# Retention attention with a Mish feed-forward layer: a new order of the first steps, and loads issued later in a visit

## The chip, the cores and the metric

The kernel runs on one core of a Trainium2 chip. The metric is device time in microseconds (us), the median of several runs. A separate execution under the hardware profiler gives the profile; its times are read against that execution's own time.

Engines are named as in the profile: PE is TensorE (matrix products; PEld its weight loads), DVE is VectorE, ACT is ScalarE, POOL is GpSimd, SP is SyncE, which here only issues DMAs. "L371" is line 371 of the kernel's file.

## The reference

Two stages are computed. The first is retention: per batch and head, scores q k^T / sqrt(64) are multiplied by a decay mask and then with v. The second takes the result as 4608 tokens of 512 features through a feed-forward layer with Mish, h tanh(softplus(h)).

```python
def _attn_ref(q, k, v):                 # (8, 8, 576, 64) each
    scores = scale * np.matmul(q, k.transpose(0, 1, 3, 2))
    gamma = 1.0 - 2.0 ** (-5.0 - np.arange(H))
    rel = pos[:, None] - pos[None, :]
    Dmat = np.where(rel >= 0, gamma[:, None, None] ** rel[None, :, :], 0.0)
    return np.matmul(scores * Dmat[None], v)

def _moe_ref(x, w_in, w_out):           # (4608, 512), (512, 2048), (2048, 512)
    h = x @ w_in
    sp = np.where(h > 20.0, h, np.log1p(np.exp(np.minimum(h, 20.0))))
    return (h * np.tanh(sp)) @ w_out
```

## The kernel before

**Tiling.** The 4608 tokens are 36 chunks of 128, four of them (c = 4) half from one batch and half from the next. Four chunks make a tile of 512 tokens, so there are nine tiles t. The order is: first the first 128 positions of all eight batches (tiles 0 and 1, "first" chunks, numbered 0 to 7), then for each pair of batches the chunks 1 to 3 of both and the shared last one (chunks 8 to 35). A first chunk needs only the masked scores. A later chunk also needs a state, the sum of k^T v over the earlier positions of its batch.

**Order.** The schedule is written out by hand: each engine carries out its instructions in the order in which the program emits them, and waits only where data or a buffer is missing. So moving a Python line moves its instructions in the queues of all engines that it uses.

**Helpers for the first chunks** (t is 0 or 1, g the half: batches 0 and 1, or 2 and 3; i is 0 for q, 1 for k). `f_transpose(t, g, i, parts)` transposes on PE into PSUM (L194, L197) and copies to SBUF (L202) with the engine that `parts` names. `f_scores(t, g)` makes the scores of two batches on PE (L211) and multiplies each by `dmask` on VectorE (L215). `f_v(t, b, copy)` casts v of a batch to bf16 (L222). `f_out(t, b, copy)` multiplies masked scores with v (L236) and casts the result into the tile `xT` (L239). `f_state` scales v for the state (L245). `keep_warm(n, pool, name)` issues n matrix products of zeros (L167) into a PSUM buffer of a pool; nobody reads them. The pools `ps_sc` and `ps_h` have two buffers each, `ps_st` and `ps_o` one.

**Feed-forward.** `g1(t, f)` is one of 16 blocks of the first product, four matmuls (L371), with the Mish on ScalarE (L373). With `half[0]` or `half[1]` it does 256 of the 512 token columns: for tile 0 the blocks 0 to 3 are done by halves, the first half needing `xT` of batches 0 and 1 only. `g2(t, i)` is a quarter of the second product of one chunk, four matmuls (L386); `g2_first` does the same for tile 0 (L403), `g2_last` (L414) for the last chunk. `store` copies the result out of PSUM (L422) and issues the store on SP.

**Tables on ScalarE.** `dmask`, `gq` and `gv` are exponentials (Exp), `gq` and `gv` made from `ex`, which VectorE computes from `pos`; `warm` is a single Mish on one column, whose effect is that the Mish table is loaded there.

**First loads.** q of batches 0 to 3 is issued by SP (L120), k of them by POOL (L106), v by POOL in pairs of batches (L117), then w_in in four blocks (L86).

**Later chunks.** `load(n)` issues q, k and v of a chunk on POOL (L263; L267 for the shared chunks): into `qraw` (5 buffers), `qks` (9) and `vraw` (7). Steps of a chunk: P scales q on VectorE (L273), V scales v on POOL (L279, into `vs`, 5 buffers), T transposes q and k, on PE (L288, copy L289) for chunks under 18 and as a DMA transpose issued by SP (L291) from 18 on, S makes the scores (L301) and masks them (L305), O adds state and scores times v (L353, L358) and casts to `xT` (L362). `state` makes the next state (L333, L336). `load_k0(b)` loads k of a batch's first chunk again (L249).

**The main loop** (t = 2 to 9) does 16 steps per tile, in two visits of eight (w = 0 to 7). A visit works on chunks n and n+1: S at w = 0, O at w = 4, and for the next pair the V, T and P steps. Each step also does one `g1` of tile t and one `g2` of tile t-1. `more_loads(upto)` issues the loads that are still missing up to chunk `upto`, at most two; PF = 5 is how far ahead they run. In tiles 3 and 4, `load_k0` stands at the top of steps 4 and 12.

Of the kernel before, what the change touches and what calls it, by code (L numbers as in the profile page):

```python
# [17 lines left out]
def kernel(  # L18
# [29 lines left out]
    PF = 5  # L48
# [23 lines left out]
    ps_sc = ctx.enter_context(tc.tile_pool(name="ps_sc", bufs=2, space=PS))  # L72
    ps_st = ctx.enter_context(tc.tile_pool(name="ps_st", bufs=1, space=PS))
    ps_h = ctx.enter_context(tc.tile_pool(name="ps_h", bufs=2, space=PS))
    ps_o = ctx.enter_context(tc.tile_pool(name="ps_o", bufs=1, space=PS))
# [21 lines left out]
    q0 = gts[0][:, H:nF, :].bitcast(F32).rearrange("p (b a) c -> p b (a c)", a=2)  # L97
    v0 = {}
    fst = {}
# [64 lines left out]
    def keep_warm(n, pool=ps_o, name="ops"):  # L164
        idle = pool.tile([P, 512], F32, name=name)
        for _ in range(n):
            nc.tensor.matmul(idle, lhsT=zeros[:, 0:P], rhs=zeros, start=True, stop=True)  # L167
# [14 lines left out]
    def f_transpose(t, g, i, parts):  # L182

        name = ("qb", "kb")[i]
        out_t = first.tile([P, H, P], BF16, name=name + "T", bufs=2)
        n = 8 // len(parts)
        moves = []
        for j, (pool, tname, copy) in enumerate(parts):
            tp = pool.tile([P, 2, 8, P] if tname == "sc" else [P, 8, P], BF16, name=tname)
            tp = (tp[:, 0] if tname == "sc" else tp)[:, 0:n]  # L190
            for r in range(n):
                if t == 1:
                    mix = fst[1][name, "mix", g][:, n * j + r]
                    nc.tensor.transpose(tp[:, r, :], mix.rearrange("p x d -> p (x d)"), ident)  # L194
                else:
                    for x in range(2):
                        nc.tensor.transpose(tp[ds(64 * x, 64), r, :],  # L197
                                            fst[0][name][:, 2 * g + x, ts(n * j + r, D)], ident)
            moves.append((copy, out_t.rearrange("p h (g r) -> p h g r", r=8)[:, :, :, ds(n * j, n)],
                          tp.rearrange("p r (g h) -> p h g r", h=H)))  # L200
        for copy, to, src in moves:
            copy(to, src)  # L202
        fst[t][name, g] = out_t

    def f_scores(t, g, between=None):
        qT, kT = fst[t]["qb", g], fst[t]["kb", g]
        scs = [ps_sc.tile([P, 2, NP, P], F32, name="sc").rearrange("p a b i -> p (a b) i") for _ in range(2)]
        for h in range(H):
            for x in range(2):
                r = ds(64 * x, 64)  # L210
                nc.tensor.matmul(scs[x][:, h, :], lhsT=kT[r, h, :], rhs=qT[r, h, :], start=True, stop=True)  # L211
        for x in range(2):
            b = 2 * g + x
            sm = first.tile([P, H, P], BF16, name="sm0", bufs=4)
            nc.vector.tensor_tensor(sm, scs[x], dmask, op=OP.mult)  # L215
            fst[t]["sm", b] = sm
            if between and x == 0:
                between()

    def f_v(t, b, copy):  # L220
        vb = first.tile([P, H, D], BF16, name="vb", bufs=4)
        copy(vb, v0[4 * t + b])  # L222
        fst[t]["vb"][b] = vb

    def f_out(t, b, copy):
        if b == 0:
            xts[t] = xp.tile([P, KC, NCH * P], BF16, name="xT")
        vb = fst[t]["vb"][b]
        if t == 0:
            pool, name = ((ps_h, "hp"), (ps_h, "hp"), (ps_st, "st"), (ps_o, "ops"))[b]  # L230
            ot = pool.tile([P, NP, P], F32, name=name)
        else:
            ot = ps_sc.tile([P, 2, NP, P], F32, name="sc")[:, 0]
        for p in range(NP):
            for e in range(2):
                nc.tensor.matmul(ot[ds(64 * e, 64), p, :], lhsT=vb[:, 2 * p + e, :],  # L236
                                 rhs=fst[t]["sm", b][:, 2 * p + e, :],
                                 start=(p == 0), stop=True, skip_group_check=True)
        copy(xts[t][:, :, ts(b, P)], ot)  # L239
# [7 lines left out]
    def load_k0(b):  # L247
        k0[b] = first.tile([P, H, D], BF16, name="k0", bufs=B)
        nc.gpsimd.dma_start(out=k0[b], in_=k[b, :, 0:P, :].rearrange("h p d -> p h d"))  # L249
# [3 lines left out]
    def load(n):  # L253
        if n >= n_chunks:
            return
        b, c = chunks[n]
        qr = io.tile([P, H, D], F32, name="qraw")
        vr = io.tile([P, H, D], F32, name="vraw", bufs=7)
        qks = io.tile([P, 2, H, D], BF16, name="qks", bufs=9)
        live[n] = {"q": qr, "v": vr, "qks": qks}  # L260
        for t, src in ((qr, q), (qks[:, 1], k), (vr, v)):
            if c < 4:
                nc.gpsimd.dma_start(  # L263
                    out=t, in_=src[b, :, ds(P * c, P), :].rearrange("h p d -> p h d"))
            else:
                for e in range(2):
                    nc.gpsimd.dma_start(  # L267
                        out=t[ds(64 * e, 64)],
                        in_=src[b + e, :, ds(512, 64), :].rearrange("h p d -> p h d"))
# [123 lines left out]
    def stores():  # L393
        while ready:
            store(*ready.pop(), nc.vector.tensor_copy)
# [34 lines left out]
    def att(n, steps):  # L430
        if n >= n_chunks:
            return
        for step in steps:
            {"P": step_p, "V": step_v, "T": step_t, "S": step_s, "O": step_o}[step](n)

    dve, act, pool = nc.vector.tensor_copy, nc.scalar.copy, nc.gpsimd.tensor_copy
# [1 line left out]

    half = (slice(0, 2 * P), slice(2 * P, 4 * P))
    nc.scalar.activation(dmask, dmask, AX.Exp, bias=lnd[:, 0:1])  # L440
    for b in range(2):
        dve(fst[0]["qb"][:, b, :], q0[:, b, :])
    keep_warm(8)
    f_transpose(0, 0, 1, [(ps_h, "hp", act), (ps_h, "hp", dve)])
    f_transpose(0, 0, 0, [(ps_st, "st", act), (ps_o, "ops", dve)])
    for h in range(H):
        nc.vector.tensor_scalar(ex[:, :, h], pos, lg[h], None, op0=OP.mult)
    act(fst[0]["qb"][:, 2, :], q0[:, 2, :])
    f_transpose(0, 1, 1, [(ps_h, "hp", act), (ps_h, "hp", act)])
    keep_warm(2, ps_sc, "sc")  # L450
    f_scores(0, 0)
    keep_warm(3, ps_st, "st")
    f_transpose(0, 1, 0, [(ps_st, "st", act), (ps_o, "ops", act)])
    keep_warm(4, ps_h, "hp")
    nc.scalar.activation(gq, ex, AX.Exp)
    nc.scalar.activation(gv, ex, AX.Exp, scale=-1.0)
    nc.scalar.activation(warm, lnd, AX.Mish)
    f_v(0, 0, pool)
    f_v(0, 1, pool)
    f_scores(0, 1, lambda: f_out(0, 0, dve))  # L460
    f_out(0, 1, act)
    f_v(0, 2, pool)
    f_v(0, 3, act)
    keep_warm(3, ps_st, "st")
    for f in range(4):
        g1(0, f, half[0])
# [34 lines left out]
    for i in range(nF):  # L501
        for step in steps.get(i, "").split():
            n = int(step[1])
# [17 lines left out]
    def more_loads(upto):  # L521
        for _ in range(2):
            if queued[0] <= upto:
                load(queued[0])
                queued[0] += 1
# [4 lines left out]
    for u in range(24):  # L530
        j, w = divmod(u, 4)
# [32 lines left out]
    for t in range(2, nT + 1):  # L564
        for i in range(nF):
            n, w = NCH * (t + 1) + i // 8 * 2, i % 8
            if t in (3, 4) and i in (4, 12):
                load_k0(2 * t - 2 + i // 8)
            by_pe = n + 2 < NPE
            if w == 0:  # L570
                stores()
                state(n + 1)
                att(n, "S")
                att(n + 1, "S")
            if w == 4:
                state(n + 3)
                stores()
                att(n, "O")
                att(n + 1, "O")
                state(n + 3)  # L580
            if by_pe and w in (1, 3):
                att(n + 2 + w // 2, "P")
            if w in (0, 1):
                att(n + 2 + w, "V")
                more_loads(n + 2 + w + PF)
            if w - (5 if by_pe else 0) in (0, 1):
                att(n + 2 + (w == 1 or w == 6), "T")
            if w == 7 and n + 4 >= NPE:
                att(n + 4, "P")
                att(n + 5, "P")  # L590
            stores()
            if t < nT:
                g1(t, i)
            if t == 2:
                if i % 2:
                    g2(1, 8 + i // 2)
            elif t < nT or i < 12:
                g2(t - 1, i)
# [32 lines left out]
```

## Time and profile before

| what | us |
|---|---|
| three runs | 315.39, 315.41, 316.31 (median 315.41) |
| the profiled execution's own time | 317.75 |
| its span, first to last instruction | 316.0 |
| PE busy in 0 to 20 us of the span | 14.24 |
| PE busy in 20 to 40 | 19.02 |
| PE busy in 120 to 140 | 19.55 |
| PE busy in 140 to 160 | 18.78 |
| PE busy in 180 to 200 | 19.90 |

Except in the last 16 us, other stretches of 20 us hold between 19.79 and 19.90 us of PE work. The difference of 1.75 us between the profiled time and the span lies before the first and after the last recorded instruction.

How to read it. The page cuts the span into 40 slices of 7.9 us and gives each engine's busy share as a digit (9 is 90 per cent or more). PEclk is the clock that was granted to TensorE, in tenths of full speed; DMA is the busy share of the 16 DMA engines. A timeline row has the start, the duration, the engine, the line and the instruction, and in brackets how long the engine had been idle before and who released it. A matmul's recorded duration includes its drain, so a row of x16 is a little longer than the pace of the stream.

Transfers, from issue to landing: the last pair of v for tile 0 was issued at 7.1 us and took 9.3; the four blocks of w_in were issued at 6.4, 9.3, 10.1 and 10.8 and took 7.7, 9.2, 12.0 and 13.9; w_out was issued at 19.1, 20.9, 29.1 and 30.1 and took 10.8, 11.6, 8.4 and 10.1.

### The profile page before, as it was taken

How to read it: one execution, taken by the hardware profiler on the slowest of the kernel's cores; microseconds unless marked ns; L12 is line 12 of the kernel's file. 1: busy time of each engine (PE TensorE's matmuls, PEld its weight loads, DVE VectorE, ACT ScalarE, POOL GpSimd, SP SyncE). 2: the span in 40 equal slices, each digit the busy share in tenths (PEclk: the TensorE clock that was granted, in tenths of full speed). 3: DMA queues.
4: the chain of work that ended last, by engine and by line, in shares of the span. 5: the costliest groups of instructions: out<-in, count | busy, mean ns of one | idle time of the engine just before them, and what ended most of it. 6: DMA issues, size and time to landing. Idle time of an engine off the chain costs nothing.

```text
span 316.0 us, 5807 instructions
## 1 busy us (share of the span) xinstructions
PE 302.7 (96%) x2428; PEld 153.4 (49%) x2468; DVE 135.3 (43%) x198; ACT 111.7 (35%) x185; POOL 143.0 (45%) x178
## 2 busy tenths in 40 slices
PE   5779999999999999998999999999999999999995
PEld 2454554555555554544545454545454545444444
DVE  3553148487636535353535453535354332001111
ACT  3476525753353533332232333332323232333300
POOL 8587849889684976356373536252010000000000
PEclk9599999999999999999999999999999999999999
DMA  7999999999992899999999999991514000010031
GB/s 176 232 207 204 221 207 197 274 163 183 234 183 79 139 163 164 187 83 210 153 181 88 214 136 180 122 168 36 98 37 100 35 33 35 34 33 33 35 97 69
DMA packets 73642, 42.85 MB, mean 136 GB/s; under 512 B 58640, under 2 KB 64528, under 8 KB 73616
## 3 DMA queue, kind: packets, MB, share of 16 engines
q0 software_dynamic: 48640, 27.27, 64.0%
q1 hardware_dynamic: 24832, 15.08, 25.9%
q8 instruction: 19, 0.31, 0.5%
q10 hardware_dynamic: 144, 0.13, 0.1%
q14 instruction: 7, 0.06, 0.1%
HBM read 38.80 MB, written 9.44 MB: 153 GB/s over the span
## 4 chain that ended last, share of the span: by engine, by line
PE 74%; DMA 20%; POOL 3%; issue 1%; ACT 0%; DVE 0%; POOLq 0%
PE hp L371 31%; PE ops L386 26%; DMA qkT<-qks 9%; PE hp L386 4%; DMA w_out_t<-in_moe_w_out_dram 4%; DMA qraw<-in_q_dram 4%; PE sc L301 2%; DMA vraw<-in_v_dram 2%; PE st L333 2%; DMA gT<-in_k_dram 2%; PE sc L353 1%; PE sc L358 1%; PE sc L288 1%; PE hp L414 1%; POOL gT L106 1%
## 5 line engine op out<-in xcount | busy, mean ns | idle before, releaser
L371 PE MATMUL hp<-xT,w_in_t 128*128 128x512 bf16 (+1 forms) x562 | 141.4, 373 | 2.9 <-DVE xT L239 0.8
L373 ACT ACTIVATE gT<-hp 128x512 bf16<-128x512 f32 (+1 forms) x148 | 86.8, 586 | 157.7 <-PE hp L371 143.9
L386 PE MATMUL ops<-w_out_t,gT 128*128 128x512 bf16 x430 | 110.1, 379 | 0.4
L371 PEld LDWEIGHTS <-w_in_t 128*128 128x128 bf16 x592 | 55.1, 98 | 62.8 <-issue 2.1
L386 PEld LDWEIGHTS <-gT 128*128 128x128 bf16 x496 | 48.3, 98 | 58.0 <-issue 0.8
L422 DVE COPY res<-ops 128x512 f32<-128x512 f32 x28 | 19.3, 688 | 83.4 <-PE ops L386 79.6
L336 DVE TENSOR_TENSOR ssb<-st,diag 128x512 bf16<-128x512 f32 x32 | 21.9, 685 | 49.6 <-PE st L333 49.6
L263 POOL DMA_DIRECT2D qraw<-in_q_dram x24 | 22.1, 921 | 40.5 <-DVE qks L273 38.0
L279 POOL TENSOR_TENSOR vs<-vraw,gv 128x512 bf16<-128x512 f32 x28 | 29.9, 1077 | 20.2 <-issue 14.0
L305 DVE TENSOR_TENSOR sm<-sc,mask 128x1024 bf16<-128x1024 f32 x28 | 33.1, 1216 | 5.9 <-PE sc L301 5.9
L263 POOL DMA_DIRECT2D vraw<-in_v_dram x24 | 21.7, 903 | 2.6 <-DMA vpair<-in_v_dram 1.5
L263 POOL DMA_DIRECT2D qks<-in_k_dram x24 | 21.6, 899 | 1.2 <-DMA w_out_t<-in_moe_w_out_dram 0.9
L273 DVE TENSOR_TENSOR qks<-qraw,gq 128x512 bf16<-128x512 f32 x28 | 19.9, 746 | 0.0
L362 DVE CAST xT<-sc 128x512 bf16<-128x512 f32 x24 | 15.3, 680 | 0.0
L386 PE MATMUL hp<-w_out_t,gT 128*128 128x512 bf16 x61 | 14.7, 379 | 0.2
L215 DVE TENSOR_TENSOR sm<-sc,dmask 128x1024 bf16<-128x1024 f32 x8 | 9.5, 1220 | 8.4 <-PE sc L211 8.4
L289 ACT COPY qkT<-sc 128x1024 bf16<-128x1024 bf16 x10 | 10.1, 1010 | 8.0 <-PE sc L288 8.0
L267 POOL DMA_DIRECT2D qraw<-in_q_dram x8 | 5.6, 708 | 14.1 <-DVE qks L273 14.1
L301 PE MATMUL sc<-qkT 64*128 64x128 bf16 x224 | 9.4, 218 | 1.5 <-DMA qkT<-qks 1.5
L301 PEld LDWEIGHTS <-qkT 64*128 64x128 bf16 x224 | 6.3, 94 | 6.7 <-issue 3.4
L353 PE MATMUL sc<-qkT,ssb 128*64 128x128 bf16 (+1 forms) x224 | 9.5, 213 | 0.0
L358 PE MATMUL sc<-sm,vs 128*64 128x128 bf16 x192 | 9.4, 219 | 0.0
(102 smaller groups left out, 193.3 us busy)
## 6 DMA issues: line engine op xcount, KB each, us to landing
out_dram<-res SPq DMA_DIRECT2D x31, 256.0 KB, 3.9
qraw<-in_q_dram POOLq DMA_DIRECT2D x24, 256.0 KB, 5.5
vraw<-in_v_dram POOLq DMA_DIRECT2D x24, 256.0 KB, 8.3
qks<-in_k_dram POOLq DMA_DIRECT2D x24, 128.0 KB, 7.3
w_in_t<-in_moe_w_in_dram POOLq DMA_DIRECT2D x4, 512.0 KB, 10.6
w_out_t<-in_moe_w_out_dram POOLq DMA_DIRECT2D x4, 512.0 KB, 10.4
gT<-in_q_dram SPq DMA_DIRECT2D x4, 256.0 KB, 4.9
gT<-in_k_dram POOLq DMA_DIRECT2D x8, 128.0 KB, 6.9
```

Of the source, the lines that this page charges most:

```text
L263: nc.gpsimd.dma_start(out=t, in_=src[b, :, ds(P * c, P), :].rearrange("h p d -> p h d"))
L273: nc.vector.tensor_tensor(live[n]["qks"][:, 0], live[n]["q"], gq[:, c, :].unsqueeze(2).to_broadcast([P, H, D]), op=OP.mult)
L279: nc.gpsimd.tensor_tensor(vs, live[n]["v"], gv[:, c, :].unsqueeze(2).to_broadcast([P, H, D]), op=OP.mult)
L301: nc.tensor.matmul(sc[:, e, p, :], lhsT=qk[r, 1, p, :], rhs=qk[r, 0, p, :], start=True, stop=True)
L305: nc.vector.tensor_tensor(sm.rearrange("p e n i -> p (e n) i"), sc.rearrange("p e n i -> p (e n) i"), m.unsqueeze(1).to_broadcast([P, 2 * ...
L336: nc.vector.tensor_tensor(ssb.rearrange("p e n d -> p e (n d)"), st.rearrange("p n d -> p (n d)").unsqueeze(1).to_broadcast([P, 2, NP * 64 ...
L353: nc.tensor.matmul(ot[ds(64 * e, 64), p, ds(i0, iw)], lhsT=st_sb[bb, cc][:, e, p, :], rhs=qk[:, 0, p, ds(i0, iw)], start=(i0 == 0 and p == ...
L362: nc.vector.tensor_copy(xts[t][:, :, ts(s, P)], ot)
L371: nc.tensor.matmul(hp[:, cols], lhsT=w_in_t[:, c, ts(f, P)], rhs=xts[t][:, c, cols], start=(c == 0), stop=(c == KC - 1))
L373: nc.scalar.activation(gts[t][:, f, cols], hp[:, cols], AX.Mish)
L386: nc.tensor.matmul(ops, lhsT=gts[t][:, f, ts(s, P)], rhs=w_out_t[:, f, :], start=(f == 0), stop=(f == nF - 1))
L422: copy(ot, ops)
```

## The change

It has two parts. In the first steps, ScalarE's `gq`, `gv` and the Mish table come right after `dmask`, and `ex` on VectorE moves ahead with them; the casts of q for batches 0 and 1 are no longer adjacent, and the cast of batch 2 goes from ScalarE to VectorE. The scores of the first half come ahead of the second half's transposes. The v casts of batches 0 to 2 stand together, the outputs of batches 0 and 1 ahead of the second half's scores, and the cast of batch 3 goes from ScalarE to VectorE. The warm-up matmuls change from 8, 2, 3, 4, 3 to 12, 2, 3, 3. In the main loop, the calls of `more_loads` go from steps 0 and 1 to steps 4 and 5 of a visit, for the same chunks.

```diff
     half = (slice(0, 2 * P), slice(2 * P, 4 * P))
     nc.scalar.activation(dmask, dmask, AX.Exp, bias=lnd[:, 0:1])
-    for b in range(2):
-        dve(fst[0]["qb"][:, b, :], q0[:, b, :])
-    keep_warm(8)
-    f_transpose(0, 0, 1, [(ps_h, "hp", act), (ps_h, "hp", dve)])
-    f_transpose(0, 0, 0, [(ps_st, "st", act), (ps_o, "ops", dve)])
+    dve(fst[0]["qb"][:, 0, :], q0[:, 0, :])
     for h in range(H):
         nc.vector.tensor_scalar(ex[:, :, h], pos, lg[h], None, op0=OP.mult)
-    act(fst[0]["qb"][:, 2, :], q0[:, 2, :])
-    f_transpose(0, 1, 1, [(ps_h, "hp", act), (ps_h, "hp", act)])
-    keep_warm(2, ps_sc, "sc")
-    f_scores(0, 0)
-    keep_warm(3, ps_st, "st")
-    f_transpose(0, 1, 0, [(ps_st, "st", act), (ps_o, "ops", act)])
-    keep_warm(4, ps_h, "hp")
     nc.scalar.activation(gq, ex, AX.Exp)
     nc.scalar.activation(gv, ex, AX.Exp, scale=-1.0)
     nc.scalar.activation(warm, lnd, AX.Mish)
-    f_v(0, 0, pool)
-    f_v(0, 1, pool)
-    f_scores(0, 1, lambda: f_out(0, 0, dve))
+    dve(fst[0]["qb"][:, 1, :], q0[:, 1, :])
+    keep_warm(12)
+    f_transpose(0, 0, 1, [(ps_h, "hp", act), (ps_h, "hp", dve)])
+    f_transpose(0, 0, 0, [(ps_st, "st", act), (ps_o, "ops", dve)])
+    dve(fst[0]["qb"][:, 2, :], q0[:, 2, :])
+    keep_warm(2, ps_sc, "sc")
+    f_scores(0, 0)
+    f_transpose(0, 1, 1, [(ps_h, "hp", act), (ps_h, "hp", act)])
+    f_transpose(0, 1, 0, [(ps_st, "st", act), (ps_o, "ops", act)])
+    for b in range(3):
+        f_v(0, b, pool)
+    keep_warm(3, ps_h, "hp")
+    f_out(0, 0, dve)
     f_out(0, 1, act)
-    f_v(0, 2, pool)
-    f_v(0, 3, act)
+    f_scores(0, 1)
+    f_v(0, 3, dve)
     keep_warm(3, ps_st, "st")
     for f in range(4):
         g1(0, f, half[0])
...
             if w in (0, 1):
                 att(n + 2 + w, "V")
-                more_loads(n + 2 + w + PF)
+            if w in (4, 5):
+                more_loads(n + w - 2 + PF)
```

## The prediction

> **What bounds the kernel now.** I read the page first (busy shares, then the 40 slices).
>
> ```profile
> span 316.0 us, 5807 instructions
> PE 302.7 (96%) x2428; PEld 153.4 (49%) x2468; DVE 135.3 (43%) x198; ACT 111.7 (35%) x185; POOL 143.0 (45%) x178
> ...
> PE   5779999999999999998999999999999999999995
> ...
> PEclk9599999999999999999999999999999999999999
> DMA  7999999999992899999999999991514000010031
> ```
>
> TensorE sets the time: from the fourth slice on it is at 9 tenths. Its 13.3 us of idle time lie in the first three slices (0 to 23.7 us), in the tail, and in little else. So whatever makes TensorE reach its dense stream earlier shortens the run, unless data holds it later. The timeline of all engines shows the start:
>
> ```profile
> 9.82 1.06 PE L197 MATMUL hp<-ident,gT 128*64 128x128 bf16 x15 [0.41 <-DMA gT<-in_k_dram]
> ...
> 11.78 1.13 PE L211 MATMUL sc<-qbT,kbT 64*128 64x128 bf16 x16
> ...
> 12.84 1.46 PE L167 MATMUL st<-zeros 128*128 128x512 bf16 x3
> ...
> 14.36 0.64 PE L197 MATMUL st<-ident,gT 128*64 128x128 bf16 x8
> ...
> 16.33 0.62 PE L211 MATMUL sc<-qbT,kbT 64*128 64x128 bf16 x16
> 16.39 1.28 ACT L457 ACT_TABLE_LOAD   x1
> 16.43 0.62 POOL L222 CAST vb<-gT 128x512 bf16<-128x512 f32 x1 [3.31 <-DMA gT<-in_v_dram]
> ...
> 18.12 0.68 DVE L239 CAST xT<-hp 128x512 bf16<-128x512 f32 x1
> ...
> 18.95 2.10 PE L371 MATMUL hp<-xT,w_in_t 128*128 128x256 bf16 x16 [0.68 <-ACT vb L222]
> ...
> 22.41 12.71 PE L371 MATMUL hp<-xT,w_in_t 128*128 128x256 bf16 x63 [0.79 <-DVE xT L239]
> ```
>
> Columns are start, duration, engine, line, instruction. The first scores (11.78) stand behind the second half's k transposes, though their operands were copied by 9.15; the second scores (16.33) wait for a chain that starts at 14.36 only because warm-up matmuls precede it. The mark to watch is 22.41, where the second half-columns of the first layer begin. The windows view gives the clock there (the column behind the five engines):
>
> ```profile
> 8.50:8.60 0.10, 0.00 (x0) 0.00 (x0) 0.10 (x2) 0.10 (x2) 0.00 (x0) 0.75 1.32 307
> ...
> 12.00:15.00 3.00, 2.94 (x32) 1.69 (x32) 2.06 (x2) 0.00 (x0) 1.12 (x2) 0.50 1.19 256
> ...
> 15.30:15.40 0.10, 0.10 (x4) 0.05 (x2) 0.00 (x0) 0.10 (x1) 0.00 (x0) 0.61 0.57 102
> ```
>
> TensorE ran at half clock from about 8.56 to 15.38. Last, TensorE's waits after the start: two waits at the attention scores for transposes done by DMA (0.35 us at 125.95, 1.11 us at 143.26).
>
> ```profile
> PE sc L301 <- DMA qkT<-qks: 1.5, 2, 1.1
> ```
>
> **The front, step by step.** I replay the new order with the old durations, at half clock until 15.39 (**slow**) or at full clock from 11.98 (**fast**).
>
> ScalarE and VectorE. The cast of q0 for batch 0 ends at 5.30 as now; the eight ex instructions (1.03 us) follow, to 6.33. ScalarE then does gq and gv (0.38 together, 15.99 to 16.37), the table load and the warm Mish (1.49, 16.39 to 17.88): to 8.22. The first k copy, now at 7.64, starts at 8.2, the second copy ends at 9.3 against 8.71: **0.6 us lost** where that engine is the last, since VectorE's half of q^T ends at 9.15 anyway. The cast of batch 1 slips from 6.02 to about 6.35, hidden: the k of batch 1 lands at 7.2 (the transposes start at 7.19). The cast of batch 2 goes to VectorE (0.43 to 0.57 us after 9.15), hidden behind the k transposes. Of the price of the table switch the trace has 1.28 us with no gap in front. The Trainium skill, "ScalarE: Activation LUTs", section "What ACT_TABLE_LOAD costs", gives 1283 ns plus about 1380 ns of drain for a switch: by that rule the first copies would come 1.4 us later still; the rows (gv ends 16.37, load at 16.39) show no drain.
>
> The four extra warm-up matmuls (12 instead of 8) cost nothing: eight took 3.59 us from 1.26, twelve at the same 0.427 spacing end by 6.4, under the wait for k of batch 1 until 7.19.
>
> TensorE. Scores of the first half at 9.4 instead of 11.78 (1.13 us, half clock), to 10.5; their two mask products on VectorE (2.35) end at 12.9. The k and q transposes of the second half follow at once, about 0.9 us each as a stream (row of 1.06 with its drain), to 12.2; ScalarE's copies end at 13.0. Three warm-up matmuls: 1.46 slow, 0.65 fast. Outputs of batches 0 and 1: v casts on GpSimd end at 12.56 and 13.12 (first pair landed 11.9; unmoved). So batch 1's output ends at 14.7 slow, 13.5 fast, and xT is copied (0.57 on ScalarE, 0.68 on VectorE) by 15.3 or 14.1. Second scores end at 15.7 or 14.1, three warm-up matmuls follow (0.65), and the first half-columns (2.10 us) run 16.3 to 18.4, or 14.75 to 16.85; w_in's first block landed at 14.1 (issued 6.36, 7.7 to landing).
>
> Last link: the second pair of v lands at 16.43. GpSimd casts batch 2 by 17.05 as now. VectorE has its two mask products first (2.35 from 15.7 or 14.1), then the cast of batch 3 moved from ScalarE (0.6; now 18.25 to 18.87): 18.65 or 17.05. Outputs of 2 and 3 and the xT copy (0.35 to 0.4, then 0.69) end at 19.8 or 18.4. The mark goes from 22.41 to **19.85 or 18.45: gain 2.55 or 3.95 us**. Which clock? A stretch of 3.41 us ending at 11.98 held about 1.9 us of matmuls now and the clock stayed low; the next, with 3.35, raised it. The new order puts some 2.6 there, midway, so I take the middle, **3.25 us**. "TensorE: Matmul & The Clock Gate", section "Part 1: The HAM clock gate", wants a busy window of about 3.4 us; read strictly it speaks for the slow case, gain 2.55.
>
> **Is there cover behind it?** TensorE now arrives 3 to 4 us sooner at everything loaded by GpSimd, whose issues are set by queue and buffers, not by this. Tightest: w_in blocks 1, 2, 3 land at 18.6, 22.1, 24.7, needed from about 20.6, 24, 27.5; w_out block 2 at 37.5 against 43.42 now, 39.5 then; the last v pair at 44.9, its cast then due at about 45.7. The attention chunks' q and k land 46.2/47.0, 50.4/51.2, 53.6/54.9, 57.0/60.6, their transposes now run at 55.86, 60.45, 65.48, 70.51: 5 us to spare after the shift. Nothing is given back by these rows.
>
> **The loads at steps 4 and 5.** GpSimd's timeline in the later visits:
>
> ```profile
> 128.19 1.09 POOL L279 TENSOR_TENSOR vs<-vraw,gv 128x512 bf16<-128x512 f32 x1
> 137.64 0.93 POOL L263 DMA_DIRECT2D qraw<-in_q_dram  x1 [8.36 <-DVE qks L273]
> ...
> 140.35 1.07 POOL L279 TENSOR_TENSOR vs<-vraw,gv 128x512 bf16<-128x512 f32 x1
> 141.34 1.41 POOL L267 DMA_DIRECT2D qraw<-in_q_dram  x2
> ```
>
> GpSimd runs ahead and is stopped not by the visit's step but by the qraw buffer, which VectorE's q scaling frees (136.65 to 137.9). So the first load still starts at that release; only what stands between changes: v's scaling (1.07) goes ahead of both loads, so the second load comes 1 us earlier. The moved v scaling of the odd chunk now waits for the output matmuls that free its vs buffer (134.3 here), still ahead of the release. The k loads at steps 4 and 12 are thereby passed: they now stand ahead of the visit's two loads, and go out 6 to 11 us earlier (one from 127.29 to about 118.5, into the flight of the transpose that landed late at 125.9). A 256 KB load at the slices' 200 GB/s is 1.3 us of transfer. Bounds: both waits vanish (-1.5), or each late transpose gets 1.3 later (+2.6). The nearest row, two transposes already late, against one k load that comes in and one that goes out: I take **+0.4**.
>
> Beside loads the transposes took 9 to 15 us from issue to landing; at 208 and 225, with none, 3.1 to 3.6. "DMA: Bandwidth & Descriptors", section "Queues, rings and completion order", has each engine take turns between queues packet by packet, which fits that and speaks against any load that comes in.
>
> **Sum.** -3.25 + 0.4 = -2.85 us. The profiled execution took 317.75 us with a span of 316.0; its span would be 313.15 and its time 314.9. The runs' median, 315.41, lies 2.3 under that; I take off the same 2.85: **312.6 us**. Extremes: -3.95 - 1.5 gives 310.0, -2.55 + 2.6 gives 315.5.
>
> **Rivals.** (a) The loads truly leave the transposes' way, and both waits go: -3.25 - 1.46 = 310.7. For: transposes without loads land in 3 us. Against: the release above. Chance 0.08. (b) The clock falls again: with the mark at 18.45, TensorE pauses at 16.85 and 17.7, some 2.15 us of work in the 3.41 to 18.8. A window with 1.1 lost the clock, 2.75 kept it. One window at half clock loses up to 1.7: 315.41 - 3.95 + 1.7 + 0.4 = 313.6. Chance 0.10. (c) The gain is given back to a transfer I think covered, w_out block 2 with its 2 us: no change, 315.4. DMA at 9 tenths speaks for it, the landings against. 0.08. (d) **Slower.** The doubled-up loads and early k loads push DMA transposes late. Margins of the four late pairs now: -0.35, -1.1, +1.7, +0.6. A delay x at each costs x + x + (x-1.7) + (x-0.6) = 4x - 2.3; it decides against the front from x = 1.4 and gives x = 1.8 at 317.3 (4.9 lost, 3.0 gained). For: the loads come in one burst. Against: bytes don't grow, and the k loads leave other windows. Chance 0.07. Forecast: 0.67.
>
> **How the numbers follow.** What can be told from no change is about 0.3%, 0.95 us. The forecast, (a) and (b) lie under 314.46 nearly whole: faster 0.83; (c) and the edge of the forecast: same 0.10; (d) 0.07. The range 310.2 to 315.2 leaves out (d), half of (c) and the corners; the forecast's own is 310.9 to 314.4.
>
> **What would show it.** In the new trace: first scores near 9.4, table load near 6.8, second half-columns of L371 between 18.4 and 19.9 in place of 22.41, no new wait of TensorE between 23 and 100; in late visits GpSimd's qraw load still released by L273, with no v scaling between the two loads; TensorE's total wait for qkT below 4 us. A front that starts at 22, or more than 4 us of waits at L301, makes the prediction wrong.

## The result and the profile after

| kernel | runs | median us | range |
|---|---|---|---|
| before | 17 | 315.60 | 315.15 to 317.33 |
| with the change | 17 | 312.69 | 312.24 to 315.38 |

The ratio is 0.9911, with a 95% interval from 0.9893 to 0.9928: 2.3 to 3.4 us less. The forecast was 312.6. The profiled execution of the changed kernel took 313.61 us with a span of 311.9. A ratio below leaves out executions more than 1.5 per cent above the fastest one of the same kernel, which a median does not; this matters for `e4_k_behind_loads`, `e8_split_w_first` and `e11_split_again`.

The page after, top lines and slices:

```profile
span 311.9 us, 5809 instructions
PE 300.3 (96%) x2429; PEld 152.3 (49%) x2468; DVE 137.1 (44%) x200; ACT 110.7 (36%) x183; POOL 143.6 (46%) x178
...
PE   7769999999999999999999999999999999999995
...
PEclk9999999999999999999999999999999999999999
DMA  7999999999995999999996949371504100010031
```

TensorE is still what bounds the kernel. Three things differ: the first three slices hold 7, 7 and 6 tenths in place of 5, 7 and 7, the 8 in the slice from 142 to 150 us is gone, and the clock row has no 5 in its second slice. The timeline of all engines at the front (start, duration, engine, line, instruction, idle time and releaser):

```profile
6.80 1.28 ACT L446 ACT_TABLE_LOAD   x1
...
9.31 0.62 PE L211 MATMUL sc<-qbT,kbT 64*128 64x128 bf16 x16 [0.81 <-ACT qbT L202]
...
9.86 0.64 PE L197 MATMUL hp<-ident,gT 128*64 128x128 bf16 x16
...
13.56 0.62 PE L211 MATMUL sc<-qbT,kbT 64*128 64x128 bf16 x16
...
14.77 2.11 PE L371 MATMUL hp<-xT,w_in_t 128*128 128x256 bf16 x16
...
17.64 0.43 DVE L222 CAST vb<-gT 128x512 bf16<-128x512 f32 x1 [1.07 <-DMA gT<-in_v_dram]
17.67 0.87 POOL L222 CAST vb<-gT 128x512 bf16<-128x512 f32 x1 [4.51 <-DMA gT<-in_v_dram]
...
18.60 0.41 PE L236 MATMUL st<-sm,vb 128*64 128x128 bf16 x8 [1.72 <-POOL vb L222]
...
20.03 5.33 PE L371 MATMUL hp<-xT,w_in_t 128*128 128x256 bf16 x29 [0.79 <-DVE xT L239]
```

The table load is at 6.80 as forecast, and the first k copy on ScalarE follows at 8.20. The first scores start at 9.31 (11.78 before) and at full clock (0.62 us, 1.13 before), the first half-columns at 14.77 (18.95), the second half-columns at 20.03 (22.41). From 16.9 on TensorE stands still until the last v pair has landed (17.6) and is cast. That pair landed at 16.43 in the profile of before.

TensorE's waits over the whole run, complete (total, times, longest):

```profile
PE st L236 <- POOL vb L222: 1.7, 1, 1.7
PE ops L167 <- DVE zeros L125: 1.3, 1, 1.3
PE hp L236 <- POOL vb L222: 0.9, 1, 0.9
PE sc L211 <- ACT qbT L202: 0.8, 1, 0.8
PE hp L371 <- DVE xT L239: 0.8, 1, 0.8
PE hp L197 <- DMA gT<-in_k_dram: 0.6, 1, 0.6
```

All lie in the front; the two waits for DMA transposes at L301 are gone. GpSimd in a late visit:

```profile
131.20 1.04 POOL L279 TENSOR_TENSOR vs<-vraw,gv 128x512 bf16<-128x512 f32 x1 [5.47 <-PE sc L358]
132.18 0.92 POOL L249 DMA_DIRECT2D k<-in_k_dram  x1
134.68 0.89 POOL L263 DMA_DIRECT2D qraw<-in_q_dram  x1 [1.58 <-DVE qks L273]
...
137.32 1.39 POOL L267 DMA_DIRECT2D qraw<-in_q_dram  x2
```

As forecast, the first load is still released by the q scaling on VectorE (L273), no v scaling stands between the two loads, the odd chunk's v scaling now waits for the output matmuls (L358), and the k load passes both loads.

The two profiles differ by 4.1 us of span: 2.4 at the mark (22.41 to 20.03) and 1.7 behind it, 1.46 of which are the two waits. By that reading the moved loads give over a third of the gain. The experiments ask whether that holds.

### The profile page after: what moved, and what is told of

Read it like the earlier page. It is cut to its first block, busy times and chain, and to the rows that moved or that the text cites. A ratio compares the mean times of both kernels' runs of the same rounds, so it can differ in the third digit from the quotient of the medians.

```text
span 311.9 us, 5809 instructions
## 1 busy us (share of the span) xinstructions
PE 300.3 (96%) x2429; PEld 152.3 (49%) x2468; DVE 137.1 (44%) x200; ACT 110.7 (36%) x183; POOL 143.6 (46%) x178
## 4 chain that ended last, share of the span: by engine, by line
PE 92%; issue 2%; DMA 2%; POOL 2%; DVE 0%; ACT 0%; POOLq 0%; ACTq 0%
PE hp L371 39%; PE ops L386 30%; PE hp L386 4%; PE sc L301 3%; PE st L333 3%; DMA gT<-in_v_dram 2%; PE hp L403 2%; PE sc L353 2%; PE sc L358 2%; PE sc L288 1%; PE st L403 1%; PE ops L403 1%; PE hp L414 1%; POOL gT L106 1%; POOL vb L222 1%
## 5 line engine op out<-in xcount | busy, mean ns | idle before, releaser
L386 PEld LDWEIGHTS <-gT 128*128 128x128 bf16 x496 | 48.2, 98 | 58.1 <-issue 0.8
L263 POOL DMA_DIRECT2D qraw<-in_q_dram x24 | 21.8, 910 | 12.8 <-DVE qks L273 9.6
L273 DVE TENSOR_TENSOR qks<-qraw,gq 128x512 bf16<-128x512 f32 x28 | 20.2, 758 | 0.0
L362 DVE CAST xT<-sc 128x512 bf16<-128x512 f32 x24 | 15.3, 680 | 0.0
L358 PE MATMUL sc<-sm,vs 128*64 128x128 bf16 x192 | 9.4, 219 | 0.0
L301 PE MATMUL sc<-qkT 64*128 64x128 bf16 x224 | 9.0, 218 | 0.0
L403 PEld LDWEIGHTS <-gT 128*128 128x128 bf16 x64 | 5.8, 98 | 6.5
## 6 DMA issues: line engine op xcount, KB each, us to landing
w_in_t<-in_moe_w_in_dram POOLq DMA_DIRECT2D x4, 512.0 KB, 11.1
```

The lines of the kernel that those rows point to most:

```text
L263: nc.gpsimd.dma_start(out=t, in_=src[b, :, ds(P * c, P), :].rearrange("h p d -> p h d"))
L273: nc.vector.tensor_tensor(live[n]["qks"][:, 0], live[n]["q"], gq[:, c, :].unsqueeze(2).to_broadcast([P, H, D]), op=OP.mult)
L301: nc.tensor.matmul(sc[:, e, p, :], lhsT=qk[r, 1, p, :], rhs=qk[r, 0, p, :], start=True, stop=True)
L386: nc.tensor.matmul(ops, lhsT=gts[t][:, f, ts(s, P)], rhs=w_out_t[:, f, :], start=(f == 0), stop=(f == nF - 1))
L403: nc.tensor.matmul(outs[0, s], lhsT=gts[0][:, f, ts(s, P)], rhs=w_out_t[:, f, :], start=(f == 0), stop=(f == nF - 1))
```

## Experiments

### The two parts, each alone

`e1_front_alone` is the changed kernel with

```diff
             if w in (0, 1):
                 att(n + 2 + w, "V")
-            if w in (4, 5):
-                more_loads(n + w - 2 + PF)
+                more_loads(n + 2 + w + PF)
```

> The changed first steps, with the loads where they were (steps 0 and 1). Theory 1, both parts give something: the front alone gives the 2.4 us by which the second half-columns of L371 came earlier (22.41 to 20.03), so 313.2 us beside 315.6 before, and TensorE's waits for qkT at L301 stay at 1 to 2 us, the transposes landing after 9 to 15 us. Rival, the loads are inert and the waits went because the front came earlier: 312.7 us, waits under 0.3 us, transposes landing after 5 to 12 us.

`e2_loads_alone` is the kernel before with the same lines the other way round.

> The first steps as before, the loads at steps 4 and 5. Theory 1: the waits at L301 go (1.46 us in the profile of before), the transposes land after 5 to 12 us, second half-columns still at 22.4; 314.1 to 315.1 us. Rival, loads inert: 315.6 us, waits of about 1.5 us in the profile. My prediction's step (+0.4 us) would give 316.0.

| run | median us | ratio to before | interval |
|---|---|---|---|
| e1, front alone | 312.91 | 0.9918 | 0.9893 to 0.9943 |
| e2, loads alone | 316.21 | 1.0026 | 0.9997 to 1.0054 |

Kernel before on the same chip: 315.92. The front alone gives the whole gain, as far as these intervals tell; the loads alone give none: the saving of 1.5 us that the two profiles suggested lies outside e2's interval (0.1 us less to 1.7 us more). Yet e1 is no case for "inert" either, for the loads do change what they were said to change. The line of DMA issues for the transposes (count, median us to landing), first e1, then e2:

```profile
qkT<-qks SPq DMA_TRANSPOSE x18, 11.1
```

```profile
qkT<-qks SPq DMA_TRANSPOSE x18, 6.2
```

In the profiles of before and of the change the medians are 10.2 and 6.0. The whole-run median hides where the effect lies. From issue to landing, in us (lowest, median, highest of six transposes):

| profile | the six issued between 106 and 149 us | the six issued between 153 and 199 us |
|---|---|---|
| before (loads at steps 0 and 1) | 9.1, 13.4, 15.3 | 9.9, 11.1, 12.7 |
| e1 (steps 0 and 1) | 8.5, 13.1, 13.8 | 10.9, 12.0, 12.4 |
| the change (steps 4 and 5) | 9.4, 10.7, 11.8 | 4.7, 6.0, 6.9 |
| e2 (steps 4 and 5) | 7.5, 12.8, 14.3 | 5.4, 6.2, 8.5 |

The large effect is in the second column, and it is worth nothing there, because these transposes were on time already: no profile has a wait for one of them. The waits of before belong to the first column, where the moved loads change little. TensorE's wait for transposes in e1, with the loads where they always were:

```profile
PE sc L301 <- DMA qkT<-qks: 0.2, 1, 0.2
```

So the 1.46 us of waits in the profile of before are no fixed cost of the old order: they are what that one execution had (0.2 here, none in the profiles of e6 and e9, both with the old order). No theory fits whole. Theory 1 of e2 has the waits right (none in its profile) and the time wrong. Theory 1 of e1 has a time within the interval and the waits wrong (0.2 us, not 1 to 2). The rivals have the times right, but the loads are not inert, since the transposes follow them, and the waits of 1.5 us that e2's rival names did not come.

### Steps of the front

`e6_scores_alone` makes one move in the kernel before:

```diff
-    f_transpose(0, 1, 1, [(ps_h, "hp", act), (ps_h, "hp", act)])
     keep_warm(2, ps_sc, "sc")
     f_scores(0, 0)
+    f_transpose(0, 1, 1, [(ps_h, "hp", act), (ps_h, "hp", act)])
     keep_warm(3, ps_st, "st")
```

> The kernel before with one move: the first half's scores (and the two warm-up matmuls ahead of them) in front of the second half's k transposes. Theory 1, each step of the front gives a part, since behind the scores the old order still has seven warm-up matmuls and the table load ahead of the second scores: second half-columns at 21.0 to 21.6, 314.3 to 315.0 us. Rival, the scores' place carries the whole gain: 20.1 or earlier, 313.3 us or less. Rival, it gives nothing alone: 22.4, 315.7 us.

314.35 us beside 315.80, ratio 0.9950 (0.9927 to 0.9973). The timeline of TensorE:

```profile
20.93 3.39 PE L371 MATMUL hp<-xT,w_in_t 128*128 128x256 bf16 x21 [0.79 <-DVE xT L239]
```

The mark is at 20.93 and not 22.41. The scores' place alone gives 1.4 to 1.5 us, about half of the front's gain. A part of that can be the clock: in e6's profile it was at half until about 11.4 us, in that of before until 15.4. But the executions of before on this chip whose mean granted clock was 0.998 or more took 315.36 us by median, so 1.0 us is left without it. The rest of the front's gain has to come from what e6 leaves as it was; of that (the warm-up matmuls and the table load ahead of the second scores, the engines of the casts, the place of the outputs) only the cast of batch 3 is separated below.

`e7_v3_on_scalar` takes that cast back to ScalarE:

```diff
     f_scores(0, 1)
-    f_v(0, 3, dve)
+    f_v(0, 3, act)
```

> The changed kernel with the cast of v for batch 3 back on ScalarE. Theory 1, ScalarE then stands at that cast until the pair lands, with the Mish of the first half-columns behind it and their two PSUM buffers full: the first half-columns end 1 to 1.5 us later and the mark moves by about 1.2 us, 313.6 to 314.2 us. Rival, the engine of the cast makes no difference, since the pair's landing sets the time on either: 312.7 us.

313.66 us, ratio 0.9951 (0.9920 to 0.9981), 1.0 us over the changed kernel's median above and 0.5 over that of its later runs (e10). The intervals just overlap, but the lowest of its 12 runs, 313.45, lies over 1.1 us above the change's lowest (312.24, 312.33). Two answers of its trace, the timeline and TensorE's waits:

```profile
17.89 0.62 ACT L222 CAST vb<-gT 128x512 bf16<-128x512 f32 x1 [3.17 <-DMA gT<-in_v_dram]
```

```profile
PE hp L371 <- ACT gT L373: 2.6, 1, 2.6
```

ScalarE stood 3.2 us at the cast with the Mish of two ready blocks behind it, and TensorE waited 2.6 us for their PSUM buffers. Theory 1 holds: the cast itself is short on either engine (0.62 us here, 0.43 on VectorE), and what differs is who queues behind it. On VectorE it is nobody urgent. The profiled execution (317.94 us) is not typical of the time: after the pause its clock fell to half from about 19.6 to 26.5 us (the column behind the five engines):

```profile
20.00:23.40 3.40, 2.61 (x25) 1.87 (x24) 1.66 (x2) 1.32 (x3) 3.38 (x6) 0.50 1.24 206
```

`e3_eight_warm` has `keep_warm(8)` for `keep_warm(12)`.

> The changed kernel with 8 warm-up matmuls at its start in place of 12. Theory 1, the four more only keep the clock up, and what sets the second half-columns is the landing of the last v pair (17.6): the granted clock falls to half near 8.6 us, scores and transposes take about twice as long, but second half-columns start at 20.0 to 20.4: 312.7 to 313.1 us. Rival, the clock is what the front's gain hangs on: they start at 21.0 to 21.5, 313.7 to 314.2 us.

312.66 us, ratio 0.9908 (0.9880 to 0.9936): the same as with twelve. The clock column of its profile shows no fall, but the pace was slow at first (eight transposes in 0.73 us, 0.44 in the changed kernel; scores in 0.73), and full from there on:

```profile
7.86 0.73 PE L197 MATMUL st<-ident,gT 128*64 128x128 bf16 x8
...
9.92 0.73 PE L211 MATMUL sc<-qbT,kbT 64*128 64x128 bf16 x16
```

Its mark was at 18.89 all the same, since the last v pair landed at 16.5: the slow pace up to 10 us did not set it. Of its five other executions, four had a mean granted clock of 0.995 (about 3 us at half: 0.005 of 311 us, twice) and took 312.35 to 312.67 us; where their clock was low is not recorded. So the rival (313.7 us or more) does not hold, while the fall near 8.6 us that the expectation describes was not seen.

### The last v pair

`e5_v_before_w` issues that pair ahead of w_in's first block:

```diff
-    load_w_in(0, 512)
     load_first_v(2)
+    load_w_in(0, 512)
```

> The changed kernel with the last v pair of tile 0 issued ahead of the first block of w_in. Theory 1, the landing of that pair (16.4 to 17.6) sets the second half-columns: it now lands near 14.2 and the w_in block near 16.4, the first half-columns start at 16.5, not 14.8, TensorE no longer waits for vb of batch 2, and the second half-columns start at 18.6 to 18.9 in the profile: 312.2 to 312.7 us. Rival, the pair's landing is only a bystander (TensorE's order or the copies set the mark): the late w_in shifts everything by 1.7 us, mark at 20 or later, 313.8 us or more.

314.55 us, ratio 0.9963 (0.9937 to 0.9989): 1.9 over the changed kernel. Its timeline:

```profile
14.82 0.61 POOL L222 CAST vb<-gT 128x512 bf16<-128x512 f32 x1 [1.15 <-DMA gT<-in_v_dram]
...
17.98 3.16 PE L371 MATMUL hp<-xT,w_in_t 128*128 128x256 bf16 x16 [2.54 <-DMA w_in_t<-in_moe_w_in_dram]
...
22.87 1.35 PE L371 MATMUL hp<-xT,w_in_t 128*128 128x256 bf16 x9 [0.79 <-DVE xT L239]
```

The time and the mark are the rival's, yet not for its reason: the pair landed by 14.8 as expected, but w_in's block landed 10.4 us after its issue and not some 9, and TensorE stood 2.5 us before it. Waiting for one transfer was exchanged for waiting for the other, in front of more work. The half-columns took 3.16 us for 2.11 because the granted clock fell to half from 18.5 to 21.6 in this execution, the slowest of the twelve; eight executions at a mean clock of 0.998 or more took 314.05 by median. That the pair does set the mark is seen across the profiles with the change's front: mark at 18.80 and 18.89 where it landed by 16.5 (e4, e3), at 20.03 to 20.23 where it landed at 17.6 to 17.8 (the change, e1, e10).

`e8_split_w_first` keeps the early pair and needs less of w_in first:

```diff
-    load_w_in(0, 512)
     load_first_v(2)
+    load_w_in(0, 256)
     nc.gpsimd.tensor_copy(fst[0]["qb"][:, 3, :], q0[:, 3, :])
+    load_w_in(256, 256)
...
     f_out(0, 1, act)
+    f_v(0, 3, act)
     f_scores(0, 1)
-    f_v(0, 3, dve)
     keep_warm(3, ps_st, "st")
-    for f in range(4):
+    for f in range(2):
         g1(0, f, half[0])
     f_out(0, 2, act)
     f_out(0, 3, dve)
+    for f in range(2, 4):
+        g1(0, f, half[0])
```

> A candidate: the last v pair ahead of w_in, w_in's first block in two halves, v of batch 3 cast on ScalarE ahead of the second scores, outputs of batches 2 and 3 between the first half-columns of blocks 1 and 2. Theory 1 (the landings of v and of w_in's first block bound the front): second half-columns near 18.1 and the full blocks from 20.2 instead of 21.0 or later: 311.6 to 312.2 us. Rival, something else bounds it (VectorE's mask products, the clock): no better than 312.7 us.

312.27 us, ratio 0.9886 (0.9843 to 0.9929); one of six executions took 322.34. The timeline of TensorE (this kernel's lines are one higher):

```profile
15.50 1.05 PE L372 MATMUL hp<-xT,w_in_t 128*128 128x256 bf16 x8
...
17.20 0.41 PE L237 MATMUL ops<-sm,vb 128*64 128x128 bf16 x8 [0.31 <-DVE sm L216]
17.55 6.62 PE L372 MATMUL hp<-xT,w_in_t 128*128 128x256 bf16 x39
```

The half-columns now run on without a pause from 17.55. To set it beside the changed kernel on one chip, and to ask about the loads a third time, three more runs: the candidate with the loads at steps 0 and 1 (`e9_split_old_loads`), the changed kernel (`e10_change_again`), and the candidate again (`e11_split_again`).

> The candidate front (v pair ahead of w_in, split block) with the loads where they were before, at steps 0 and 1. Theory 1 (in unprofiled runs the loads' move is worth nothing on the path, because the transposes that it speeds up were in time anyway): 312.0 to 312.6 us, the same as the candidate within 0.3 us, with qkT landing after 10 to 13 us in the visits from 170 us on. Rival, the loads' move gives 1 us or more as the two profiles suggest: 313.2 us or more.

> The changed kernel itself once more, beside the candidate on one chip: 312.4 to 312.9 us; second half-columns at 18.8 when the last v pair lands at 16.4, at 20.0 when it lands at 17.6.

> The candidate once more. If the landings bounded the front: 0.3 to 0.6 us under the changed kernel on the same chip, 312.0 to 312.4 us. Rival, no better: within 0.2 us of it.

| run | median us | ratio to before | interval |
|---|---|---|---|
| e9, candidate, old loads | 312.39 | 0.9902 | 0.9884 to 0.9919 |
| e10, the change | 313.16 | 0.9929 | 0.9908 to 0.9949 |
| e11, candidate | 312.42 | 0.9914 | 0.9883 to 0.9944 |

The candidate lies 0.7 us under the change by medians, with either place of the loads, and e8 by 0.4 under the change's first runs, but the intervals of the ratios overlap: that it is better is not beyond doubt. e9 and e11 agree to 0.03 us by medians: again nothing can be told of the loads' place.

e10 shows more: its profiled execution took 316.22 us. Windows of it; the column behind the five engines is the granted clock:

```profile
18.70:19.30 0.60, 0.57 (x16) 0.48 (x16) 0.00 (x0) 0.11 (x1) 0.60 (x2) 0.88 1.23 205
19.30:19.60 0.30, 0.14 (x4) 0.00 (x0) 0.12 (x1) 0.30 (x1) 0.30 (x1) 0.50 1.25 208
...
25.00:26.00 1.00, 1.00 (x4) 0.35 (x3) 0.00 (x0) 0.43 (x1) 0.37 (x1) 0.51 1.24 201
```

The v pair was late again (10.6 us to landing), TensorE paused from 16.9 to 18.7, and the clock then fell to half from 19.2 to 26. The end of the first layer of tile 0 is where the next transposes start; TensorE's timeline of e10 and of the changed kernel's first profile:

```profile
35.15 0.61 PE L194 MATMUL sc<-ident,qbx 128*128 128x128 bf16 x8
```

```profile
32.53 0.61 PE L194 MATMUL sc<-ident,qbx 128*128 128x128 bf16 x8
```

From nearly the same mark (20.23 and 20.03) e10 is 2.6 us later: 0.2 from the mark, 2.4 from the clock. e1's profile has the same with a shorter stretch (half clock from 20.0 to 23.4, 1.2 us lost). This is the rival of the prediction on the clock, seen in two of the four profiled executions whose front is the change's as it stands (e1 and e10; not in the change's first profile, nor in e4, where the pair landed early). e5 and e7 had it too, behind longer pauses of 2.5 and 2.6 us.

`e12_warm_in_pause` tries to bridge that pause:

```diff
+    keep_warm(4)
     f_out(0, 2, act)
     f_out(0, 3, dve)
```

> The changed kernel with four more warm-up matmuls between the first half-columns and the outputs of batches 2 and 3, where TensorE waits for the last v pair. Theory 1, the pause there is what loses the clock in some executions (half clock from 19.2 or 20.0 us on in two profiles, 1.2 and 2.4 us lost): the clock stays full behind the pause, runs over 314 us become rare (at most 1 of 12), the median stays at 312.6 to 313.0 us, the four costing 0 to 0.3 us when the pair lands early. Rival, the clock is lost for another reason: it falls as often, 3 or more of 12 runs over 314 us.

313.77 us, ratio 0.9940 (0.9913 to 0.9967); the clock stayed full in its profile, but 3 of 8 executions were over 314 (none over 314.9). The four matmuls move the outputs from 17.4 to 17.83 where the pair lands early, which is 0.4 us; the median rose by more, for a reason that stays open. Of the three executions over 314, two had a mean granted clock of 0.999 and 1.00, so a lost clock is not what made them long. Seven of the eight had 0.999 or more, against 21 of 29 (0.998 or more) of the change itself: too few to say that the clock was kept more often. Neither expectation fits.

### The place of the k loads

`e4_k_behind_loads` gives GpSimd the change's order except that `load_k0` falls behind the two loads again:

```diff
             if w in (0, 1):
                 att(n + 2 + w, "V")
-            if w in (4, 5):
-                more_loads(n + w - 2 + PF)
+            if w == 1:
+                more_loads(n + 2 + PF)
+                more_loads(n + 3 + PF)
```

> The changed kernel with both loads of a visit emitted at step 1, behind both v scalings: GpSimd's order is that of the change except that the four k loads of tiles 3 and 4 stand behind the visit's two loads again, as before. Theory 1a, it is the k loads' place that freed the transposes: waits at L301 of 0.5 us or more come back, transposes in visits with a k load land after 10 us or more, 313.2 to 314.0 us. Rival 1b, it is the v scaling between the loads: no wait at L301 over 0.3 us, 312.7 us.

The median of all eight is 316.96 us. The ratio, without the four longest, is 0.9931 (0.9891 to 0.9971), the change's within the interval; three executions lie at 312.7 to 313.0, the other five at 315.7 to 319.8. The profile fell among these, with one long wait for a transpose:

```profile
PE sc L301 <- DMA qkT<-qks: 3.8, 1, 3.8
```

It looks like the answer to the question, and is not: the profile of e11, where the k loads stand ahead, has the same wait with 5.4 us:

```profile
PE sc L302 <- DMA qkT<-qks: 5.4, 1, 5.4
```

In both it is the first pair of DMA transposes, issued near 106 us, and TensorE's granted clock fell to half at 124 to 125 us, during the wait. Five of eight executions at 315.3 us or more, against three of 29 of the change, suggest that the k loads' place makes it more frequent; that those executions had this wait is not recorded, so the cause stays open.

## Why the prediction was right, point by point

**Total.** -2.85 us was forecast, -2.9 measured by medians and -2.8 by the ratio. The parts: front -3.25 forecast, -3.0 measured by medians and -2.6 by the ratio (e1; interval 1.8 to 3.4 less); loads +0.4 forecast, +0.3 and +0.8 alone (e2; interval -0.1 to +1.7), and nothing to be told in the pairs e1 and the change, e9 and e11.

**The front's mechanism** held: the operands were ready and the order alone kept the scores back (e6), and what was forecast to hide under other work did (the four more warm-up matmuls: 312.69 with them, 312.66 without; no new wait between 23 and 100 us). The front's size was right by the balance of errors, which is luck. The clock was taken midway between two cases and was better than both in the profile: it never fell. The half clock of before, from which both cases start, was itself not fixed: on each of the four chips the executions of before with a mean granted clock of 0.989, as in its profile, took 0.3 to 0.5 us more by median than those at 0.998 or more. (Where the clock was low is recorded for the profiled one only.) The landing of the last v pair was taken as fixed at 16.43; it was 16.4 to 16.5 in the profiles of e3 and e4, but 17.6 to 17.9 in those of the change, e1, e7 and e10, so their mark came at 20.0 and more, outside the forecast 18.4 to 19.9. And GpSimd's cast, taken at 0.62 us, took 0.87 beside VectorE's. No drain showed at the table load: gv ended at 6.78, the table load ran from 6.80 to 8.08, and the copy followed at 8.20.

**The cast of batch 3**, taken as 0.6 us moved to another engine, is worth more: back on ScalarE it costs 0.5 to 1.0 us by medians (e7), for the queue behind it. The prediction named only its end time.

**The loads.** Three things that it names are in the trace as it names them: release by L273, no v scaling between, k loads ahead. The step that failed is what follows from it: early k loads and a burst were to make late transposes later. In the profile of the change none is later: the first six land after 10.7 us by median instead of 13.4, the next six after 6.0 instead of 11.1. The time did not follow, since the second six had not been waited for. The +0.4 was a choice between two bounds; e2 leaves it possible, and zero too, but its reason was wrong. One of the bounds was also too wide: it priced a late transpose by a load of 256 KB, and the k loads that go out early are of 128 KB (0.65 us at the same 200 GB/s, an estimate). Rival (a) had the direction of the transposes right, and its 1.5 us was read off one execution.

**Rival (b)**, the clock falling in the pause, was given 1.7 us and a chance of 0.10: it occurred in two profiled executions of this front, for 1.2 and 2.4 us, and does not show in the median. **Rivals (c) and (d)**: nothing was given back to a transfer behind 23 us, and the four late pairs were not delayed in the profile of the change. But what (d) fears happens in single executions with the loads at steps 4 and 5: TensorE waited 1.1 us for a transpose in e3's profile, 0.5 in e7's and 5.4 in e11's (319.76 us). Whether it is more frequent there than in the old order, whose profiles have waits of 1.5 and 0.2 us, the record does not show.

## What to carry to other kernels

Where engines run in a written order, replay the new order with the old durations and ask at each link which input is last; the replay of some forty instructions gave the gain within a few tenths here, though two inputs (the clock and a landing) differed from the replay in opposite directions. A wait in one profile is the wait of one execution: before a gain is read off it, a second profile (or the part alone, timed) should show that it recurs. And when a cast or copy waits for a transfer, what counts is the queue behind it, not its own duration.

## What the runs showed of the hardware that was not expected

The same load, issued at 7.1 us behind the same transfers, took 9.3 us to land in some executions (before, e3, e4) and 10.5 to 10.7 in others (the change, e1, e7, e10).

When GpSimd and VectorE start a cast of the same shape (128x512, fp32 to bf16) within 0.03 us, one of them keeps the time that it has alone (0.62 us on GpSimd, 0.43 on VectorE) and the other takes 0.87. In the change and e10, where VectorE starts first, and in e3 and e4, where both rows show the same start, GpSimd's is the long one; in e12, where GpSimd starts first (16.63 against 16.65), VectorE's is.

A pause of 1.8 us (16.9 to 18.7) was followed by half clock in e10, and in the changed kernel's first profile the same pause lost nothing.

The clock column shows 1.00 ahead of the first recorded step of the clock even where the pace says half: the first warm-up matmuls, 0.43 us apart, stand under a 1.00, and later the same instructions go 0.21 us apart (three in 0.82 us, four in 1.03).
